# Four of sixteen rows that one DMA engine loads alone are spread over four engines

## Chip, cores, metric

One core of one Trainium2 chip. The metric is the device time of one execution in microseconds (us), median of several executions. Faster or slower needs 2%; for anything smaller I give the ratio of the runs with its 95% interval.

## The reference, cut to what matters

The program is a decode step for four tokens: `x + A(xn) + B(xn)` with `xn = layernorm(x)`. A is attention over a window of 2048 positions of a key and value cache (16 KV heads, 67 MB of keys and values). B ends in a two-layer MLP, and only its last product matters here:

```python
h2 = _gelu(_layernorm(x1, axis=-1) @ w3) @ w4     # w3: 576 x 4608, w4: 4608 x 576, bfloat16
return x1 + h2
```

Everything is read once: 87 MB from HBM for four rows of output.

## The kernel before: the parts concerned

The MLP's hidden vector is contracted over w4's 4608 rows. 4480 rows sit in a tile of 35 slices with 128 partitions, loaded over all 16 DMA engines (16 increments of each piece's semaphore in the trace). The last 128 rows (from `X0`) are split off into a tile x and loaded with few partitions on purpose, so that only some DMA engines work on them (in the trace the semaphore of the load of 20 partitions rises five times, that of the 12 three times, that of a one-partition load once). One row is 576 x 2 = 1152 bytes. A V block is one of the 16 loads of the value cache.

```python
XB, XC, XA = 0, 4, 5          # column slots of the x tile: 4 slots for B, 1 for C, 5 for A
XS, NX = 10, 20

def x4_rows(part):
    t = w_tiles["x4"]
    if part == "A":            # 100 rows: 20 partitions x 5 rows
        src = B_w4[X0 + 28:F, :].rearrange("(q g i) n -> g q (i n)", q=4, g=5)
        nc.sync.dma_start(out=t[0:NX, XA * D:XS * D], in_=src)
    elif part == "C":          # 12 rows: 12 partitions x 1 row
        src = B_w4[X0 + 16:X0 + 28, :].rearrange("(q g) n -> g q n", q=4)
        nc.sync.dma_start(out=t[0:12, XC * D:XA * D], in_=src)
    else:                      # 16 rows in pieces of ONE partition (q), rows lo to hi of its four
        q, lo, hi = part
        src = B_w4[X0 + 4 * q + lo:X0 + 4 * q + hi, :].rearrange("(q i) n -> q (i n)", q=1)
        nc.sync.dma_start(out=t[q:q + 1, (XB + lo) * D:(XB + hi) * D], in_=src)

# which pieces are issued after which V block:
X_AFTER = {13: ["A", (0, 0, 4)], 14: [(1, 0, 4), (2, 0, 2), "C"], 15: [(2, 2, 4), (3, 0, 2), (3, 2, 4)]}
...
# the end of the program on TensorE (cut)
mlp_extra(XC, XS)              # 12 matmuls on x (slots C and A), before the last V block
for s in range(NSL):
    pv(hl, s)                  # last V block
... o_turn, o_sum, o_spread, o_pick ...
mlp_extra(XB, XC)              # 8 matmuls on x: the 16 rows
o_proj(hl)
for lo, hi in pieces:          # w4, six pieces of 18, 6, 5, 4, 1, 1 slices
    mlp_out(lo, hi)
```

## Time and profile before

| | before |
|---|---|
| time, median (three runs) | 211.94 us (211.3 to 212.01) |
| profiled run, span | 211.41 us, 209.6 us |
| share of DMA engines, whole span | 97.7% for the one data queue |
| busiest compute engine | PE, 72% |
| last landing of w4's last piece | 206.60 us |
| copy of the result starts | 206.96 us |

The DMA engines hardly rest (a share of 1.00 or 1.01 from 100 to 204 us), so the time is set by when the last of them has landed its last byte, and by the few matmuls and the store after that. The trace lists every DMA packet with start, duration and bytes, but not its engine. In this document a **train** is a sequence of packets linked by their times, each starting 3 to 4 ns before the record of the one ahead of it ends; there are 16, and I take each for one engine. "Lowest" and "second" to "fifth" are my names for the five trains with x rows, the lowest being the one with the one-partition loads and the fifth the one with the 20-partition load alone; the trace doesn't number engines. Sums of trains are my working from these records, not rows of the profile's page.

### The profile page before, as it was taken

Reading aid. Unit: us, or ns where it says so; the run is one execution under the profiler, and the core shown is the slowest. Engines: PE = TensorE matmul, PEld = TensorE weight load, DVE = VectorE, ACT = ScalarE, POOL = GpSimd, SP = SyncE. Lnnn points to the kernel's source line nnn. Section 1 sums busy time; section 2 is a strip of 40 time slices with the busy share of each in tenths; the row PEclk is TensorE's granted clock in tenths of the full one; section 3 lists DMA queues with packets and bytes.
Section 4 is the critical chain, followed back from the end, with each engine's and each line's share of the span. In section 5 each row is a group of like instructions: output and inputs, shape, how many; then the busy total and the mean of one; then the engine's idle time right before and its main releaser. Section 6 shows DMA issues by size and latency. Waiting matters only on the chain.

```text
span 209.6 us, 2356 instructions
## 1 busy us (share of the span) xinstructions
PE 150.2 (72%) x958; PEld 58.2 (28%) x972; DVE 113.4 (54%) x156; ACT 34.8 (17%) x72; POOL 9.0 (4%) x32
## 2 busy tenths in 40 slices
PE   0357297699590039958998987589697955999693
PEld 0122132233140003213444332234232312343361
DVE  4511877894910083935608889176848390764200
ACT  7612201012010011110222221102111111023100
POOL 4710000000000000000002100000000000000000
PEclk9999589999787555788999999789978796699979
DMA  7999999999999999999999999999999999999992
GB/s 301 400 419 425 425 424 430 438 432 424 434 450 406 427 435 420 443 428 435 428 428 435 419 428 434 435 425 438 428 428 438 415 439 435 416 441 428 432 403 98
DMA packets 6702, 87.31 MB, mean 417 GB/s; under 512 B 758, under 2 KB 1034, under 8 KB 1700
## 3 DMA queue, kind: packets, MB, share of 16 engines
q1 hardware_dynamic: 6684, 87.17, 97.7%
q8 instruction: 7, 0.11, 0.2%
q10 hardware_dynamic: 8, 0.00, 0.0%
q14 instruction: 3, 0.02, 0.0%
HBM read 87.17 MB, written 0.00 MB: 416 GB/s over the span
## 4 chain that ended last, share of the span: by engine, by line
DMA 66%; DVE 15%; PE 14%; ACT 1%; issue 1%; SPq 1%; DVEq 0%; ACTq 0%
DMA kn<-in_A_k_cache_dram 43%; DVE kt L253 12%; DMA vn<-in_A_v_cache_dram 10%; DMA w_sb<-in_B_w_dram 7%; DMA wq_sb<-in_A_wq_dram 6%; PE S L366 5%; PE g_ps L496 2%; PE q_ps L310 2%; PE O L423 1%; PE oT L436 1%; DVE PT L400 1%; PE acc L212 1%; DVE mx L372 1%; PE S L388 1%; ACT E L395 1%
## 5 line engine op out<-in xcount | busy, mean ns | idle before, releaser
L366 PE MATMUL S<-kt,qz 128*128 128x512 bf16 x242 | 76.4, 437 | 32.2 <-DVE kt L253 30.4
L253 DVE STREAM_TRANSPOSE kt<-kn 128x2048 int32<-128x2048 int32 x32 | 73.4, 2297 | 24.3 <-DMA kn<-in_A_k_cache_dram 22.9
L366 PEld LDWEIGHTS <-qz 128*128 128x128 bf16 x256 | 23.5, 106 | 64.3 <-issue 47.7
L423 PE MATMUL O<-vn,PT 128*32 128x512 bf16 x256 | 23.9, 414 | 9.3 <-DMA vn<-in_A_v_cache_dram 9.3
L430 ACT ACTIVATE O_sb<-O,rd 128x512 f32<-128x512 f32 x16 | 11.0, 686 | 64.7 <-DVE rd L413 48.3
L395 ACT ACTIVATE E<-S 128x512 bf16<-128x512 f32 x16 | 9.5, 597 | 72.6 <-PE S L388 72.6
L400 DVE STREAM_TRANSPOSE PT<-E 128x512 bf16<-128x512 bf16 x16 | 11.4, 710 | 14.4 <-ACT E L395 14.4
L446 DVE TENSOR_REDUCE on<-oT 128x8 bf16<-128x128 f32 x16 | 4.6, 289 | 22.1 <-PE oT L436 21.9
L423 PEld LDWEIGHTS <-PT 128*32 128x32 bf16 x256 | 5.5, 95 | 33.0 <-issue 22.1
L436 PE MATMUL oT<-ident_w,O_sb 128*128 128x128 f32 x64 | 12.7, 331 | 0.3 <-ACT O_sb L430 0.3
L372 DVE TENSOR_REDUCE mx<-S 128x1 f32<-128x512 f32 x16 | 10.5, 659 | 1.1 <-PE S L366 1.1
L436 PEld LDWEIGHTS oT<-ident_w,O_sb 128*128 128x128 f32 x64 | 8.3, 165 | 5.2 <-issue 4.3
L388 PE MATMUL S<-nm,j_row 8*128 8x512 bf16 x16 | 6.7, 421 | 1.8 <-DVE nm L384 1.7
L354 PE MATMUL S<-negbig,ohT 4*128 4x512 bf16 x16 | 6.2, 384 | 0.0
L212 PE MATMUL acc<-w_sb,gT 128*4 128x288 bf16 x70 | 5.5, 311 | 0.6 <-DMA w_sb<-in_B_w_dram 0.6
L310 PE MATMUL q_ps<-wq_sb,xnT 128*32 128x512 bf16 x40 | 4.3, 611 | 2.2 <-DMA wq_sb<-in_A_wq_dram 2.2
L212 PE MATMUL acc<-wo_sb,op 128*4 128x288 bf16 x64 | 5.5, 324 | 0.4 <-DVE op L468 0.4
L496 PE MATMUL g_ps<-w_sb,ln2T 128*32 128x512 bf16 (+2 forms) x55 | 5.5, 441 | 0.0
L212 PEld LDWEIGHTS <-gT 128*4 128x4 bf16 (+3 forms) x90 | 4.2, 89 | 3.1 <-issue 1.0
L538 POOL TENSOR_TENSOR g_u<-g_x 128x180 f32<-128x180 f32 x1 | 0.5, 486 | 101.9 <-ACT g_x L532 101.9
L681 DVE CAST fin<-acc 4x288 bf16<-4x288 f32 x1 | 0.4, 446 | 8.1 <-PE acc L212 8.1
L534 DVE COPY g_x<-gT_ps 128x64 f32<-128x64 f32 x2 | 0.4, 223 | 7.5 <-PE gT_ps L518 7.5
(94 smaller groups left out, 79.3 us busy)
## 6 DMA issues: line engine op xcount, KB each, us to landing
kn<-in_A_k_cache_dram SPq DMA_DIRECT2D x16, 2048.0 KB, 25.9
vn<-in_A_v_cache_dram SPq DMA_DIRECT2D x16, 2048.0 KB, 22.7
wo_sb<-in_A_wo_dram SPq DMA_DIRECT2D x4, 1152.0 KB, 37.8
w_sb<-in_B_w_dram SPq DMA_DIRECT2D x1, 4608.0 KB
wq_sb<-in_A_wq_dram SPq DMA_DIRECT2D x1, 4096.0 KB
w_sb<-in_B_w_dram SPq DMA_DIRECT2D x1, 2592.0 KB, 11.0
w_sb<-in_B_w_dram SPq DMA_DIRECT2D x2, 576.0 KB, 34.3
w_sb<-in_B_w_dram SPq DMA_DIRECT2D x1, 864.0 KB
```

Of the source, the lines that this page charges most:

```text
L212: nc.tensor.matmul(out=acc_of(i), lhsT=lhsT, rhs=rhs[:, i * CW:(i + 1) * CW], start=False, stop=False, skip_group_check=True)
L253: nc.vector.transpose(out=kt[:], in_=src)
L310: nc.tensor.matmul(out=q_ps[r][g * QD:(g + 1) * QD, :], lhsT=xnT[:, k, :], rhs=wq_sb[:, col:col + NW], start=(j == 0), stop=False, skip_gr ...
L366: nc.tensor.matmul(out=S_ps[h][:], lhsT=qz[:, z0:z0 + P], rhs=kt[:, ib, c0:c0 + SC, e:2 * QD:2].rearrange("p c k -> p (c k)"), start=False ...
L372: nc.vector.reduce_max(out=mx[:], in_=S_ps[h][:], axis=AX.X)
L388: nc.tensor.matmul(out=S_ps[h][:], lhsT=j_row[:], rhs=st.pop(("nm", h))[:, 0:1].to_broadcast([NJ, NW]), start=False, stop=False, skip_grou ...
L395: nc.scalar.activation(out=E[h][:].rearrange("p c k -> p (c k)"), in_=S_ps.pop(h)[:], func=ACT.Exp, scale=scale, accum_out=st["rs"][:, h % ...
L400: nc.vector.transpose(out=PT[h][:], in_=E.pop(h)[:])
L423: nc.tensor.matmul(out=O_ps[h][g * QD:(g + 1) * QD], lhsT=PT[h][:, c, :], rhs=vn[:, :, c, :], start=(s == 0), stop=False, skip_group_check ...
L430: nc.scalar.activation(out=O_sb[h][:], in_=O_ps.pop(h)[:], func=ACT.Copy, scale=st.pop(("rd", h)))
L436: nc.tensor.transpose(out=oT[:, s, :], in_=o[:, s, :], identity=ident_w[:, s * NJ:s * NJ + P])
L496: nc.tensor.matmul(out=out, lhsT=ln2T[:, k, :], rhs=rhs, start=(j == 0), stop=False, skip_group_check=True)
```

## The change

Intent: the 16 rows ride on one engine only. Four of them (the last row of each partition) shall come by a single load over four engines, one row each, so that the lowest engine has less to do.

```diff
+        elif part == "B":
+            src = B_w4[X0:X0 + 16, :].rearrange("(q i) n -> q i n", q=4)[:, 3]
+            nc.sync.dma_start(out=t[0:4, (XB + 3) * D:XC * D], in_=src)
...
-    X_AFTER = {13: ["A", (0, 0, 4)], 14: [(1, 0, 4), (2, 0, 2), "C"], 15: [(2, 2, 4), (3, 0, 2), (3, 2, 4)]}
+    X_AFTER = {13: ["A", (0, 0, 3)], 14: [(1, 0, 3), "B", "C"], 15: [(2, 0, 3), (3, 0, 1), (3, 1, 3)]}
```

## The prediction

> **What bounds the kernel now.** I read the page's shares first, then its rows over the span, then the table by stretches, the chain of waits, the issue order of the DMA queue, and last the trace's single packet records.
>
> ```profile
> PE 150.2 (72%) x958; PEld 58.2 (28%) x972; DVE 113.4 (54%) x156; ACT 34.8 (17%) x72; POOL 9.0 (4%) x32
> DMA  7999999999999999999999999999999999999992
> DMA packets 6702, 87.31 MB, mean 417 GB/s; under 512 B 758, under 2 KB 1034, under 8 KB 1700
> q1 hardware_dynamic: 6684, 87.17, 97.7%
> q8 instruction: 7, 0.11, 0.2%
> ```
>
> No compute engine is above 72%, while the row of DMA shares is 9 in every slice but the first and the last: one queue's packets fill 97.7% of 16 engines' time over the span. The same by stretches (columns: stretch, its length, busy time of PE, PEld, DVE, ACT, POOL, granted clock, share of the 16 DMA engines, GB/s):
>
> ```profile
> 100.00:140.00 40.00, 34.61 (x250) 14.38 (x248) 24.52 (x31) 7.77 (x24) 2.30 (x5) 0.96 1.01 430
> 140.00:180.00 40.00, 30.91 (x161) 11.07 (x164) 24.70 (x33) 5.50 (x12) 0.00 (x0) 0.85 1.01 430
> 180.00:204.00 24.00, 21.86 (x209) 10.28 (x212) 10.58 (x20) 4.12 (x8) 0.00 (x0) 0.89 1.00 424
> 204.00:206.00 2.00, 1.39 (x22) 0.77 (x18) 0.00 (x0) 0.00 (x0) 0.00 (x0) 1.00 0.82 316
> 206.00:209.60 3.60, 0.93 (x12) 0.44 (x11) 0.45 (x1) 0.40 (x1) 0.00 (x0) 0.92 0.02 7
> ```
>
> From 100 to 204 us the DMA share is 1.00 or 1.01; then it falls to 0.82: some engines have run out of work while others still have some. That ragged last stretch is the only place where moving bytes between DMA engines can pay. The chain of waits agrees (columns: start, duration, what):
>
> ```profile
> 167.94 21.71 DMA vn<-in_A_v_cache_dram
> ...
> 191.35 14.53 DMA w_sb<-in_B_w_dram
> 205.88 0.04 issue
> 205.92 1.05 PE acc L212 x12
> 206.97 0.43 DVE fin L681
> ```
>
> The end is the landing of w4's last pieces, a few matmuls, one copy, and the store. The 16 rows in question are part of x, the small tile that holds w4's last 128 rows; this is who reads it and when:
>
> ```profile
> L212 PE MATMUL acc<-x,gT x20: 278/280/282, 193.0 to 198.2; 20*4 20x288 bf16 x10, 4*4 4x288 bf16 x8, 12*4 12x288 bf16 x2
> L171 SPq DMA_DIRECT2D x<-in_B_w_dram x6: 226/242/426, 164.2 to 185.3; - x6
> ```
>
> The 16 rows come by six loads of one partition each, issued from 164.2 to 185.3 us. The eight matmuls that read them run at 197.86 to 198.5 us (timeline), so what matters is not when these rows land but which DMA engine spends time on them.
>
> **The packet records.** The trace gives start, duration and bytes of every packet, but not its engine. On one engine the next packet starts about 4 ns before the record of the last one ends (after a 4-byte completion packet, 3 ns), so I linked packets into 16 trains by these ends. A few ties of 1 ns leave which train is which uncertain; the times at which trains end are certain. Three readings:
> - All 16 trains run from about 2 us to their ends with next to no gap. Each DMA engine is therefore busy throughout, and its end is the sum of its packets.
> - The last eight-packet piece of w4 (1152 B a row) ends between 204.45 and 206.30 us over the 16 trains, a spread of 1.85 us. The last seven ends are 206.08, 206.08, 206.09, 206.12 or 206.13, 206.21 and 206.30, within the uncertainty of the ties.
> - The train with the one-partition loads (packets of 4608 B at 183.43 and 188.47 us, 2304 B at 188.65, 193.80, 193.90 and 193.99) ends, as I link it, at 206.21: second to last. The train that ends at 206.30 has none of the x rows in it.
>
> The last increments of the last piece's semaphore come at 206.43, 206.51, 206.51 and 206.60 us, 0.30 us after the trains' ends; the matmuls that wait for it start at 206.64. So the end is set by a train at 206.30 that isn't the one which the change relieves, with the relieved one 0.09 us ahead of it.
>
> [...] the load of 20 partitions from 5 groups shows as 4 packets of 5760 B on each of five trains, the one of 12 partitions as 4 packets of 1152 B on each of three, and the one-partition loads lie in one train. So the new load, 4 partitions from 4 groups, should put one packet on each of four engines. [...] here a 16384-byte packet recurs every 607 ns, 27.0 GB/s[...]. [...] the trace shows seven such packets on queue 8, of 0.88 to 1.00 us where data packets of that size take 0.61. They are load on engines that the kernel didn't plan, and no part of the change.
>
> **The change, part by part.** Bytes, matmuls and the x tile's layout stay the same. There are eight x loads before and eight after, and comparing the instruction orders shows everything outside the DMA queue unchanged but for line numbers. On the DMA queue the loads stand in the same places; each of them and of w4's six loads still waits for the completion of the one eight places earlier.
>
> Removed from the lowest engine: two packets of 4608 B and four of 2304 B. Their pitches are 174 and 89 ns (a 178 ns or 93 ns record less the 4 ns overlap): 2 x 174 + 4 x 89 = 704 ns. Added: three rows at a time three times (3456 B; a line through 1152 B at 47 ns and 4608 B at 174 ns gives 132 ns), two rows once (89), one row once (47), and its row of the spread load (47): 3 x 132 + 89 + 47 + 47 = 579 ns. Completion packets: six before, six after. So the lowest engine is relieved of **125 ns**. This is three rows' worth and not four, because the spread load gives one row back.
>
> Added on the next three engines: one packet of 47 ns and one completion packet of about 6 ns net, **+53 ns each**. These are trains with the 20-partition load; I link their ends at 205.58, 205.95, 206.08 and 206.13 at the latest, so 206.18 at most afterwards. Those are still ahead of 206.30.
>
> Sum on the path: the relieved train goes from 206.21 to about 206.09, the three others to at most 206.18, the last stays at 206.30. The time won is **0**. If ties misled me and the relieved train was the last one, the gain would be the 0.09 us down to the next. After the last landing, 209.59 - 206.60 = 2.99 us follow unchanged.
>
> **Rivals.** (a) *The lowest engine sets the end and the full relief shows*: -0.13 us, 211.8. For: it carries 40 extra rows (16 + 4 + 20), some 1.9 us more than engines with none. Against: its train isn't last in this trace, and others lie within 0.1 to 0.2 us. (b) *The spread load creates a wait*: it completes when four engines have reached it rather than one, and w4's third load waits for that completion. For: engines are up to 1.8 us apart. Against: its predecessor landed at 188.7 us, w4's third load is issued at 190.9, and the packets of that load don't start before about 202 us; even 5 us late would be covered. 211.9. (c) *The queue's issue time grows*: the 12-partition load took 0.82 us to issue, one-partition loads about 0.24 (median). At most 0.6 us more on a queue that stands waiting for 4.6 us next to it, and whose transfers are queued several us ahead. 211.9. (d) *One of the three loaded engines becomes last*: +0.05 us at most, 212.0. (e) *Run-to-run drift*: the three runs span 211.3 to 212.01, 0.7 us, several times any of these.
>
> **Range and chances.** The predicted time is 211.9 us: the median of before with a change of 0 to -0.1. The mechanism can give only -0.13 to +0.05, so the range comes from the spread of the runs, widened a little for another chip: 211.2 to 212.5. A change of 2% would be 4.2 us, thirty times what the moved packets weigh. Within 2%: 0.98; faster 0.01; slower 0.01.
>
> **What would show it right or wrong.** Right: DMA shares of 9 throughout; four packets of 1152 B at about the same time on four trains, three of 3456 B on one; that train ending some 0.12 us earlier relative to the others; the last landing at 206.6 within a few tenths and 3.0 us after it. Wrong: a gap in the trains around 185 to 195 us, a longer wait of the DMA queue on the new load's line, matmuls on x later than 198 us, or a last landing that moves by over half a microsecond with the train of the one-partition loads as its cause.

What is cut there (marked) gave a rule for how a load is shared out over engines, a rated speed of one engine and a mechanism for the instruction packets; no trace of this case shows these. The sum came to 0 us won, with 0.125 us less on the lowest engine and 0.053 us more on each of the next three. That the new load puts one packet on each of four engines rests on the pattern of the loads of 20 partitions in five groups, 12 in three and of one, on five, three and one trains. The "seven such packets" are the seven of 16384 bytes that the page gives as `q8 instruction`.

## The result, and the profile after

| | before | after |
|---|---|---|
| time, median of six runs each | 211.34 us (211.07 to 212.01) | 211.31 us (211.13 to 211.79) |
| profiled run, span | 211.41, 209.6 us | 211.31, 209.5 us |
| last landing of w4's last piece | 206.60 us | 206.54 us |
| copy of the result starts | 206.96 us | 206.90 us |

The ratio is 0.9994, 95% interval 0.9974 to 1.0015: no difference. (A ratio is the mean time of one kernel's fast runs over the mean of the other's of the same rounds, so not quite the ratio of the medians in the table.)

The page of the kernel after, DMA shares and packets:

```profile
DMA  7999999999999999999999999999999999999992
DMA packets 6708, 87.31 MB, mean 417 GB/s; under 512 B 761, under 2 KB 1042, under 8 KB 1706
```

The shares are as before, digit for digit. There are six packets more: six data packets have become nine, and the load over four engines brings four completion packets where a one-partition load had one. The table by stretches (columns as in the prediction) and the chain of waits, after:

```profile
204.00:206.00 2.00, 0.93 (x14) 0.55 (x15) 0.00 (x0) 0.00 (x0) 0.00 (x0) 1.00 0.76 294
206.00:209.60 3.60, 0.86 (x12) 0.40 (x8) 0.45 (x1) 0.40 (x1) 0.00 (x0) 0.87 0.01 5
```

```profile
166.64 22.96 DMA vn<-in_A_v_cache_dram
...
191.30 14.51 DMA w_sb<-in_B_w_dram
205.81 0.04 issue
205.85 1.06 PE acc L215 x12
206.91 0.43 DVE fin L684
```

The same chain with every step within 0.07 us from w4's landing on. The ragged last stretch, where some engines have finished and others haven't, is still there (share 0.76 against 0.82). Who reads the x tile, after:

```profile
L215 PE MATMUL acc<-x,gT x20: 278/280/282, 192.8 to 199.2; 20*4 20x288 bf16 x10, 4*4 4x288 bf16 x8, 12*4 12x288 bf16 x2
L174 SPq DMA_DIRECT2D x<-in_B_w_dram x5: 240/249/427, 164.0 to 185.3; - x5
L167 SPq DMA_DIRECT2D x<-in_B_w_dram x1: 248/248/248, 170.0 to 170.0; - x1
```

Five one-partition loads and one load over four partitions (L167), which cost the queue 0.248 us to issue, 0.022 more than the piece it replaced (0.226).

The packets show the mechanism at work. Two engines can be told by their packets, and I follow their trains from the first packet of the 20-partition load to the end of the last w4 packet: the lowest one (it alone has the one-partition pieces), and, in the kernels with a spread load, the fourth (it has a packet of the spread load, and none of the 12-partition load). Ties of 1 ns leave second ways open; for the lowest train before, one would end at 206.116, but without its 2304-byte packet of 193.993 us. In the kernel before, the fourth isn't marked: two trains have a part of the 20-partition load and none of the smaller x loads. One of them, which starts at 182.639, has a 20736-byte packet of 1047 ns instead of 771. In the seven traces with a spread load that were linked, such a packet (1047 to 1061 ns) lies in the fifth train, the one with the 20-partition load alone; so I take the other one for the fourth.

| train | kernel | first x packet | end | length |
|---|---|---|---|---|
| lowest | before | 182.557 | 206.212 | 23.655 us |
| lowest | after | 182.422 | 205.949 | 23.527 us |
| fourth | before (taken for it) | 183.373 | 206.093 | 22.720 us |
| fourth | after | 183.447 | 206.220 | 22.773 us |

The lowest train is shorter by 0.128 us and the fourth longer by 0.053 us. The fourth is now the last of all 16; of the 0.127 us by which it ends later, 0.053 are the new row and 0.074 its later start in this run. So the relief is real and worth nothing: the engine that got relief wasn't the last one, and in this trace one that paid for it is. A landing is signalled about 0.3 us after its train's end (0.27 to 0.32 in eight traces here, 0.46 in one, that of the x rows early).

### The profile page after: what moved, and what is told of

It is laid out like the page before. It is cut to its first block, busy times and chain, and to the rows that moved or that the text cites. A ratio compares the mean times of both kernels' runs of the same rounds, so it can differ in the third digit from the quotient of the medians.

```text
span 209.5 us, 2370 instructions
## 1 busy us (share of the span) xinstructions
PE 150.2 (72%) x972; PEld 57.8 (28%) x972; DVE 113.3 (54%) x156; ACT 34.9 (17%) x72; POOL 9.0 (4%) x32
## 2 busy tenths in 40 slices
DMA packets 6708, 87.31 MB, mean 417 GB/s; under 512 B 761, under 2 KB 1042, under 8 KB 1706
## 4 chain that ended last, share of the span: by engine, by line
DMA 76%; PE 18%; DVE 3%; ACT 1%; SPq 1%; issue 1%; DVEq 0%; ACTq 0%
DMA vn<-in_A_v_cache_dram 51%; DMA kn<-in_A_k_cache_dram 12%; DMA w_sb<-in_B_w_dram 7%; DMA wq_sb<-in_A_wq_dram 6%; PE S L369 6%; PE O L426 3%; PE g_ps L499 2%; DVE kt L256 2%; PE q_ps L313 2%; PE oT L439 1%; PE acc L215 1%; PE S L391 1%; DVE qz L345 1%; PE gT_ps L521 1%; SPq L153 1%
## 5 line engine op out<-in xcount | busy, mean ns | idle before, releaser
L369 PE MATMUL S<-kt,qz 128*128 128x512 bf16 x256 | 77.6, 432 | 31.6 <-DVE kt L256 31.6
L215 PE MATMUL acc<-w_sb,gT 128*4 128x288 bf16 x70 | 4.9, 286 | 1.1 <-DMA w_sb<-in_B_w_dram 1.1
L215 PE MATMUL acc<-wo_sb,op 128*4 128x288 bf16 x64 | 4.6, 286 | 0.4 <-DVE op L471 0.4
L240 PE MATMUL tp<-ident_bf,first 4*128 4x4 bf16 x8 | 0.6, 172 | 5.3 <-DVE first L227 5.3
```

The source lines that it names most:

```text
L215: nc.tensor.matmul(out=acc_of(i), lhsT=lhsT, rhs=rhs[:, i * CW:(i + 1) * CW], start=False, stop=False, skip_group_check=True)
L369: nc.tensor.matmul(out=S_ps[h][:], lhsT=qz[:, z0:z0 + P], rhs=kt[:, ib, c0:c0 + SC, e:2 * QD:2].rearrange("p c k -> p (c k)"), start=False ...
```

## Experiments

**Theory.** The end follows the slowest of 16 trains, and these are nearly even: relieving one wins nothing, loading one costs as soon as it becomes the slowest. **Rivals:** the lowest engine's train alone sets the end; or only the sum of bytes counts. Later a third came up: TensorE, not DMA, sets the end in some runs. All experiments start from the changed kernel; their ratios are to the kernel before of the same rounds.

**The changed kernel again.** No edit.

> The changed kernel once more, as the null for the runs beside it. Slowest-train theory (the last of 16 DMA trains sets the end, and the lowest engine's isn't it): ratio to before 0.999 to 1.001, last landing at 206.4 to 206.7 us. Lowest-engine theory (the relieved train sets the end): 0.9994, a difference of 0.13 us, which time alone can hardly separate from the other; so the trace is to say where the train with the 3456-byte packets ends (205.95 us in the first trace of this kernel, 0.26 us ahead of the last train).

Measured: 211.33 us (211.10 to 212.02, five runs), ratio 0.9998 (0.9985 to 1.0012). The profiled run was the slow one, 212.02. Its lowest train is 23.528 us long and its fourth 22.773, the same as in the first trace to a nanosecond, and the fourth, at 206.365, is again the last by far; the last two increments of the last piece's semaphore come at 206.280 and 206.668 us. So the two lengths are properties of the kernel, and where a train stands when its x packets begin is what varies, by 0.1 to 0.2 us between these traces.

This run is 0.7 us slower than the first trace's, and the later landing gives only 0.13 of it. TensorE's order of time after the last V block has landed, and the table by stretches, first for the changed kernel's quick run (211.31 us), then for this one (212.02 us); columns of the first: start, duration, engine, line, what, and in brackets the idle time before and what ended it:

```profile
194.66 1.59 PE L426 MATMUL O<-vn,PT 128*32 128x512 bf16 x16 [0.99 <-DMA vn<-in_A_v_cache_dram]
...
200.89 3.11 PE L215 MATMUL acc<-w_sb,gT 128*4 128x288 bf16 x48
204.44 0.78 PE L215 MATMUL acc<-w_sb,gT 128*4 128x288 bf16 x10 [0.44 <-DMA w_sb<-in_B_w_dram]
205.85 1.02 PE L215 MATMUL acc<-w_sb,gT 128*4 128x288 bf16 x12 [0.63 <-DMA w_sb<-in_B_w_dram]
206.90 0.45 DVE L684 CAST fin<-acc 4x288 bf16<-4x288 f32 x1 [7.04 <-PE acc L215]
```

```profile
194.00:204.00 10.00, 8.57 (x104) 5.33 (x105) 1.43 (x4) 0.69 (x1) 0.00 (x0) 0.83 0.98 410
```

```profile
194.75 1.90 PE L426 MATMUL O<-vn,PT 128*32 128x512 bf16 x16 [1.43 <-DMA vn<-in_A_v_cache_dram]
...
200.34 2.08 PE L215 MATMUL acc<-wo_sb,op 128*4 128x288 bf16 x16
202.22 5.32 PE L215 MATMUL acc<-w_sb,gT 128*4 128x288 bf16 x70
207.57 0.45 DVE L684 CAST fin<-acc 4x288 bf16<-4x288 f32 x1 [7.29 <-PE acc L215]
```

```profile
194.00:204.00 10.00, 8.87 (x72) 4.72 (x74) 1.43 (x4) 0.69 (x1) 0.00 (x0) 0.50 0.97 410
```

In the quick run TensorE had half its clock for 3.4 us of this stretch (mean 0.83), ran ahead of w4's pieces and waited for DMA twice. In the slow run it had half its clock from 193.7 to 204.0 us, as the trace's clock record says (mean 0.50); then its 70 matmuls on w4 run in one piece without a wait, and the copy starts 0.90 us after the last landing instead of 0.36. There the end of the program is TensorE's. This trace's half-clock stretches last 3.413, 6.827, 10.240 or, once, 17.067 us, one to five times 3.413 (the last stretch is cut off by the end), and where they fall differs from run to run: in the quick run the one in this stretch lies from 195.02 to 198.43 us.

**Seventeen more rows on the lowest engine.**

```diff
+        elif part == "E":      # 17 partitions: in the trace all 17 packets on one train
+            src = B_w4[0:17, :].rearrange("(q i) n -> q (i n)", q=17)
+            nc.sync.dma_start(out=t[0:17, XS * D:(XS + 1) * D], in_=src)
...
-    ... 15: [(2, 0, 3), (3, 0, 1), (3, 1, 3)]}
+    ... 15: [(2, 0, 3), (3, 0, 3), "E"]}
```

> The changed kernel plus one load of 17 rows that goes to one engine alone: 17 packets of 1152 B at 47 ns, 0.80 us more on the lowest engine (two other pieces are merged so that the number of loads stays). Slowest-train theory: the lowest train goes from about 205.95 to 206.75 us and becomes the last; with the others at 206.2 to 206.3 the time rises by 0.4 to 0.6 us, ratio 1.002 to 1.003. Bytes theory (only the sum of bytes over 16 engines counts): 19.6 KB at 430 GB/s are 0.05 us, ratio 1.000. Lowest-engine theory: the full 0.80 us, ratio 1.004.

Measured: 212.22 us (212.01 to 212.42), ratio 1.0045 (1.0033 to 1.0058), +0.93 us in the medians. The lowest train is 24.323 us long, 0.796 more than in the changed kernel, as worked out, and is the last at 207.139 us, far from the next landing:

```profile
191.11 15.60 DMA w_sb<-in_B_w_dram
206.71 0.04 issue
206.76 1.05 PE acc L218 x12
207.81 0.43 DVE fin L687
```

The bytes theory is out: 19.6 KB, 0.02% of the traffic, cost 0.45% of the time. The size of my slack was wrong: I had taken 0.3 us between the lowest train and the last from one trace of the changed kernel, and in this run the lowest train's x packets began 0.39 us later than there (182.816), so nothing was left of it. Whether that is so in all five runs, which lie close together, the one trace can't say. By its size this result fits the lowest-engine theory just as well; the next run decides.

**No x rows at all** (wrong result: the tile is zeroed, no load of the 128 rows is issued).

```diff
+        nc.gpsimd.memset(w_tiles["x4"][0:NX, 0:XS * D], 0.0)
...
-    X_AFTER = {13: ["A", (0, 0, 3)], 14: [(1, 0, 3), "B", "C"], 15: [(2, 0, 3), (3, 0, 1), (3, 1, 3)]}
+    X_AFTER = {13: [], 14: [], 15: []}
```

> The changed kernel without any of the loads of the last 128 rows of w4; the tile is set to zero, so the result is wrong on purpose. The lowest engine is relieved of 37 rows, about 1.8 us, the next four of 1.0 to 1.25 us. Slowest-train theory: the trains that carry an instruction block and none of these rows still end at 206.1 to 206.3, so the time falls by 0 to 0.1 us, ratio 0.9995 to 1.000. Bytes theory: 147 KB at 430 GB/s, 0.34 us less, ratio 0.998. Lowest-engine theory: it falls until the next train, several tenths at least, ratio 0.997 or less.

Measured: 211.13 us (211.05 to 211.60), ratio 0.9998 (0.9985 to 1.0010). Taking 37 rows off the lowest engine and 147 KB off the whole brought nothing that five rounds can see. The 16 increments of the last piece's semaphore, one for each engine, in us (from the trace's semaphore records):

```
before        204.81 204.96 205.08 205.14 205.91 206.17 206.21 206.34 206.36 206.37 206.40 206.42 206.43 206.51 206.51 206.60
after         204.56 204.62 204.77 205.03 205.70 206.12 206.13 206.21 206.21 206.24 206.25 206.35 206.40 206.41 206.51 206.54
no x rows     204.90 204.93 204.96 204.97 205.00 205.02 205.20 205.65 205.78 206.22 206.38 206.47 206.57 206.60 206.61 206.80
four16_again  204.50 204.58 204.68 204.91 206.11 206.12 206.17 206.17 206.18 206.23 206.27 206.28 206.33 206.34 206.38 206.74
```

Without the x rows five engines have moved to 205.8 us or earlier, and the last seven stand at 206.2 to 206.8; those of before stand at 206.4 to 206.6. The instruction queue carries seven packets of 16 KiB in this trace, as in that of before, and seven is also the number of late engines. My links put the seven packets into different late trains, but over that length ties make single links uncertain. What is certain: the x rows fill the low engines up to where seven engines end anyway. This excludes the lowest-engine theory.

**All sixteen rows over four engines.**

```diff
+        elif part in ("B0", "B1", "B2"):
+            i = int(part[1])
+            src = B_w4[X0:X0 + 16, :].rearrange("(q i) n -> q i n", q=4)[:, i]
+            nc.sync.dma_start(out=t[0:4, (XB + i) * D:(XB + i + 1) * D], in_=src)
...
+    X_AFTER = {13: ["A", "B0"], 14: ["B1", "B", "C"], 15: ["B2"]}
```

> The change carried to its end: all 16 rows come by four loads over four engines. Against the changed kernel the lowest engine loses another 0.40 us (579 + 36 ns of packets and completions become 4 x 53), the next three gain 3 x 53 = 0.16 us each. Slowest-train theory: the three end at up to 206.2 + 0.16, the rest where they were: the time changes by 0 to +0.15 us, ratio 1.000 to 1.001. Lowest-engine theory: 0.5 us less than before, ratio 0.9975.

Measured: 211.92 us (211.43 to 212.15), ratio 1.0029 (1.0016 to 1.0041). Slower by more than I allowed. The last train ends at 206.422 us. It has packets of the four spread loads and of the 12-partition load, so it is the second or third engine's; the fourth train ends at 206.071. The profiled run (212.02) was again one with half clock up to 203.8 us, so that the copy started at 207.48, 0.77 us after the last landing. A mix of both, then.

> The 16 rows over four engines once more, unchanged. If the first result was chance (more runs with an unlucky half-clock stretch), the runs fall into two groups near 211.4 and 212.0 and the ratio comes down, 1.000 to 1.002. If the four loads cause it, 1.002 to 1.004 again.

Measured: 211.76 us (211.57 to 211.79), ratio 1.0009 (0.9990 to 1.0028). In this trace the fourth train is 22.931 us long, 0.211 more than the 22.720 taken for it before; worked out were 4 packets of 47 ns with 4 completions of 6 ns, 0.212. It ends at 206.415 us, and as the last row of the list above shows, its increment comes 0.36 us after the fifteenth. TensorE waits for it as in the quick run:

```profile
190.40 15.59 DMA w_sb<-in_B_w_dram
205.99 0.04 issue
206.03 1.08 PE acc L219 x12
207.11 0.44 DVE fin L688
```

So with the change carried further, one of the three trains that it loads is the slowest in both traces, by 0.33 and 0.36 us. The two results (1.0029 and 1.0009) have overlapping intervals; that the time rises by about the 0.2 us of the train is likely, not shown by the times alone.

**The x rows early** (an attempt at a better version): all x loads go ahead of the last V load, and their last eight matmuls move to the wait before the last V block.

```diff
-    X_AFTER = {... 14: [(1, 0, 3), "B", "C"], 15: [(2, 0, 3), (3, 0, 1), (3, 1, 3)]}
+    X_AFTER = {... 14: [(1, 0, 3), "B", "C", (2, 0, 3), (3, 0, 1), (3, 1, 3)], 15: []}
...
-    mlp_extra(XC, XS)
+    mlp_extra(XB, XS)
...
-    mlp_extra(XB, XC)
```

> The changed kernel with all loads of the small tile ahead of the last V load, and its eight late matmuls done with the other twelve, before the last V block's matmuls. Tail theory (the end is the later of two: the last DMA landing, or TensorE's chain from the last V landing, which a half-clock stretch from 194 to 204 us makes 0.67 us longer than the DMA, as in the profiled run of 212.02 us): the eight matmuls, 0.65 us at full and 1.12 us at half clock, fall into a wait of TensorE of 1.0 to 1.4 us; runs near 212.0 go away, the quick ones stay: all runs within 211.0 to 211.6, ratio to before 0.997 to 1.000. Slowest-train theory alone: nothing changes, the spread of the runs stays at 211.1 to 212.0.

Measured: 211.65 us (211.22 to 212.08, six runs), ratio 1.0006 (0.9985 to 1.0027). The matmuls did move into the wait, but the runs near 212 stayed, so the tail theory isn't the whole of the spread. The profiled run was 212.08, and it was slow by DMA:

```profile
192.73 1.39 PE L215 MATMUL acc<-x,gT 4*4 4x288 bf16 x20
194.59 1.41 PE L426 MATMUL O<-vn,PT 128*32 128x512 bf16 x16 [0.47 <-DMA vn<-in_A_v_cache_dram]
...
206.56 1.02 PE L215 MATMUL acc<-w_sb,gT 128*4 128x288 bf16 x12 [0.62 <-DMA w_sb<-in_B_w_dram]
```

One train without any x row ended at 206.80 us, 0.55 after the next; its landing came at 207.26 us, the fifteenth at 206.57. It is the train with the instruction block of 198.63 us, and the packet behind that block took 1321 ns instead of 771. But the packets behind this block lost about as much in the quick run (724 and 354 ns instead of 262 each), so why the train fell behind in this run I can't say. The same reordering with all sixteen rows over four engines:

> The 16 rows over four engines in four loads, with the same reordering. Tail theory: the 0.63 us that the 16 rows over four engines cost came from TensorE's chain at half clock, so it shrinks to the DMA share, 0 to 0.2 us: ratio 0.998 to 1.001. If the four-engine loads themselves cost it (three trains longer, loads issued earlier), the ratio stays at 1.002 to 1.004.

Measured: 211.60 us (211.34 to 212.00, six runs), ratio 1.0006 (0.9985 to 1.0026). The ratio lies where the tail theory put it, but the same version without the reordering had 1.0009 in the same rounds, so the reordering isn't shown to be the cause. In the trace (211.60 us) the fourth train is 22.931 us long again and the last, at 206.353. Neither version beats the kernel before.

**Sixty-eight more rows on the lowest engine.** As with seventeen, but four rows for each of the 17 partitions.

> The changed kernel plus one load of 68 rows (17 packets of 4608 B at 174 ns, 78 KB) on one engine alone: 2.96 us more on the lowest engine. Slowest-train theory: the lowest train goes from about 205.95 to 208.9 us, 2.6 to 2.7 us past the others; time +2.5 to +2.8 us, ratio 1.012 to 1.013, and a last stretch of nearly 3 us with one engine in sixteen busy. Bytes theory: 0.18 us, ratio 1.001. If the lowest engine had slack of its own beyond what the trains show, less than 2.5 us.

Measured: 216.39 us (215.80 to 216.62, four runs), ratio 1.0223 (1.0203 to 1.0243): +4.6 us, far more than the 2.5 to 2.8 expected. The direction is that of the theory, the size isn't. The table by stretches and the chain of waits of this run:

```profile
194.00:200.00 6.00, 4.34 (x56) 2.50 (x57) 1.43 (x4) 0.69 (x1) 0.00 (x0) 1.00 0.99 389
206.00:209.00 3.00, 3.00 (x28) 1.70 (x26) 0.00 (x0) 0.00 (x0) 0.00 (x0) 0.50 0.12 47
```

```profile
189.56 15.48 DMA w_sb<-in_B_w_dram
205.05 0.04 issue
205.09 7.10 PE acc L218 x70
212.19 0.43 DVE fin L687
```

Two things add up. First, of the 17 packets the first eight took 178 ns and the other nine 181 to 384, so the load took 4.13 us instead of 2.96, and in the same moments some 40 packets of other engines were slowed too (over 776 ns instead of 771; the first line shows 389 GB/s, where the kernel before moved 413). The last landing came at 210.95 us, 4.3 us later than usual. Second, w4's first piece, 36 of the last 70 matmuls, waits for the same engine and landed at 205.05 instead of 200.6; all 70 matmuls came after it, and with half the clock for much of that time (0.50 in the second line) they took 7.1 us, so the copy began 1.2 us after the last landing instead of 0.4. My expectation had priced a late train by its end alone; it also delays every piece before the last, and with them TensorE.

Why the packets were slow I tried to settle with other source rows, then other destination partitions.

```diff
-            src = B_w4[0:68, :].rearrange(...)
+            src = B_w4[X0 - 68:X0, :].rearrange(...)          # low68_far
-            nc.sync.dma_start(out=t[0:17, ...], in_=src)
+            nc.sync.dma_start(out=t[8:25, ...], in_=src)      # low68_shift (source rows as at first)
```

> The 68-row load on the lowest engine again, now of rows of w4 other than those which all engines read at that moment. If reading the same region slowed the packets (nine of 17 took 181 to 384 ns instead of 178, and some 40 of the big packets on other engines more than 776 instead of 771): all 17 take 178 ns, the lowest train is 2.96 us longer, the last landing comes at 206.6 + 2.7 = 209.3 us and the time is 2.7 us more at full clock, up to 3.6 if TensorE runs the last 70 matmuls at half clock; ratio 1.013 to 1.017. If the slow packets have another cause: 1.022 as before.

Measured: 215.89 us (215.50 to 216.23), ratio 1.0206 (1.0183 to 1.0230), and the same durations again: eight of 178 ns, then 315, 315, 182, 305, 376, 340, 213, 294, 406. The source rows aren't the cause.

> The 68-row load once more, from the first rows again, but written to partitions 8 to 24 instead of 0 to 16. In both earlier runs the packets for partitions 0 to 7 took 178 ns and the nine after them 181 to 406, in the same pattern. If the destination partition decides, the slow pattern (about 313, 314, 181, 324, 384, 349, 219, 295, 382) comes with the first nine packets now. If it is the moment (the ninth packet and later, from about 195.3 us), the first eight take 178 ns again and the next nine are slow. The time is 215 to 217 us in either case.

Measured: 216.68 us in one run (before: 211.41). Now the first four took 178 ns, and the next thirteen 319, 315, 186, 327, 382, 351, 214, 306, 398, 366, 211, 315, 380. Neither expectation: partitions 8 to 11 were slow before and are quick here, the slow packets begin with the fifth instead of the ninth, and at 194.6 us instead of 195.2 to 195.5. Taken in order of partitions, the slow packets come in fours in all three runs, begin at a partition divisible by four (8, 8 and 12), and the third of each four is the quickest (181 and 219, 182 and 213, 186, 214 and 211 ns). What slows them stays open; which other engines wrote to the same partitions just then wasn't looked at.

**512 more rows over all 16 engines.** Again the same edit with `q=128` partitions and four rows each.

> The changed kernel plus one load of 512 rows (128 packets of 4608 B, 590 KB) over all 16 engines: 8 packets of 174 ns and a completion, 1.40 us more on every engine. Slowest-train theory and bytes theory both expect +1.4 us (590 KB at 430 GB/s are 1.37 us), ratio 1.0065; it is here to set 7.5 times the bytes of the 68-row run beside that run: if only the slowest train counts, these bytes cost half as much. If DMA weren't the bound at all, 0 for both.

Measured: 212.82 us (212.57 to 212.93, four runs), ratio 1.0056 (1.0039 to 1.0074); the last landing came at 208.06 us, 1.4 to 1.5 later than the 206.54 and 206.67 of the changed kernel's two traces. The load shows as 142 packets more than the changed kernel has (6850 against 6708): 128 of data and 16 completions, less two of a merged piece. So 590 KB over all engines cost 1.1 us and 78 KB on one engine 4.6 (of which, from the numbers above, some 1.2 are the slow packets and 0.9 TensorE's later copy). This confirms DMA as the bound, and that it is a bound by engine.

**The 128 rows loaded like all others**, over all 16 engines (right result; w4 as 36 slices, no x tile).

```diff
-    NFM = NF - 1
+    NFM = NF
-            n = NFH - e
+            n = NFH
-    mlp_extra(XC, XS)
-    mlp_extra(XB, XC)
     (and the x columns of the hidden vector dropped from the transposes)
```

> The last 128 rows of w4 are loaded like the others, one per partition over all 16 engines, and multiplied by two matmuls instead of twenty; no separate tile; the result is right. The five low engines are relieved of all x rows (1.0 to 1.8 us), every engine gets 8 x 1152 B more in packets that grow from 6912 to 8064 B, 8 x 42 = 0.34 us. Slowest-train theory: the trains with an instruction block end 0.34 us later, time +0.25 to +0.35 us, ratio 1.001 to 1.002. Bytes theory: the same bytes, ratio 1.000. Lowest-engine theory: a gain of 0.5 us or more, ratio 0.9975.

Measured: 211.74 us (211.52 to 211.84), ratio 1.0005 (0.9992 to 1.0018). By time undecided between +0.15% and nothing. By trace as expected: the first nine increments of the last piece come between 205.23 and 206.00 us, the last seven between 206.60 and 207.04; the last seven come 0.24 to 0.38 us later than without x rows, about the 0.34 us of their share, and the five relieved ones don't count.

## Why the prediction was right

**DMA engines as the bound**: right. Shares, gapless trains and the 512-row run agree; in two traces (the changed kernel again, and all sixteen rows over four engines for the first time) TensorE at half clock comes last instead, by 0.4 to 0.5 us, which the prediction didn't see. It had noted a wait of TensorE for w4's last pieces, but not how short it is: 0.6 us.

**The lowest engine is relieved of 125 ns**: right. 23.655 - 23.527 = 0.128 us, and 0.127 in the second trace.

**The next three get 53 ns each**: right where it could be followed, on the fourth engine: 22.773 - 22.720 = 0.053, and 4 x 53 in the run with four such loads (0.211). The before value rests on which train I take for the fourth.

**Which train is last**: here a step failed without consequence. The prediction had "the three others to at most 206.18, the last stays at 206.30", from one trace of before. In five traces with spread loads (the changed kernel twice, all sixteen rows over four engines three times) the last train is one of the three that these loads lengthen, at 206.22 to 206.42: the fourth in four of them, the second or third in one. With the x rows early the fourth is second, at 206.25. That is rival (d), priced at +0.05 us at most. The order of trains within 0.3 us changes from run to run, and one trace was too little to say which is last. The sum is 0 to 0.05 us either way, which intervals of 0.3 to 0.4 us to either side don't resolve.

**Rival (a)**, the lowest engine alone: excluded by the run without x rows, which took 37 rows off it for 0.9998. **Rival (b)**, a wait for the spread load's completion: no such wait; w4's third load was issued at 190.83 us after, 190.88 before. The spread load did complete later: its four increments come at 188.64 to 189.68 us, where the piece it replaced landed at 189.15 (the prediction's 188.7 is the end of its packet). That leaves 1.15 us. **Rival (c)**, issue time: 0.248 us for the new load, 0.226 for the old. **Rival (e)**, drift: two sources found, a half-clock stretch of TensorE over the tail and a straggling train, each worth 0.5 to 0.7 us in one run; the share of each over all runs isn't known.

**A sign of being wrong that came true**: the prediction named matmuls on x later than 198 us, and the last eight ran from 198.87 us (before: 197.86). The rows aren't the cause, they had landed by 194.8; TensorE had half its clock from 195.02 to 198.43 us in this run, and only from 198.75 on in the trace of the kernel before. The end didn't feel it, since TensorE still waited for w4 afterwards.

**The time**: 211.9 predicted, 211.31 measured, in the range; the kernel before came down by as much with three more runs (211.94 to 211.34), so the 0.6 us are drift and not the change.

## What to carry to other kernels

Where the DMA engines have no gaps, ask of a load not how many bytes it moves but which engines carry it and whether one of them is the last to finish; relief for another engine was worth nothing here (0.128 us of it, ratio 0.9994), and load on the last cost in full (0.80 us more in its train, 0.93 us in time), with 68 rows also through what waited on its earlier pieces. Before balancing by hundreds of bytes, see how far the order of the engines' ends changes between runs: here by 0.3 us, more than the 0.13 at stake. And TensorE, which waited for DMA by only 0.6 us, was a second bound here: in the two traces where its clock was 0.50 to 0.52 up to 204 us it came last, by 0.4 to 0.5 us.

## What else the packets and the clock record showed

- 16384-byte packets follow each other every 607 ns, 27.0 GB/s, and 1152-byte ones every 47 ns, 24.5 GB/s. A fixed part of some 5 ns for each packet and 0.0368 ns for each byte fit the sizes 1152 and 4608 (47 and 174 ns).
- How many engines a load used here: 17 partitions put all 17 packets on one train, 4 on four trains, 12 (from 3 groups) on three, 20 (from 5 groups) on five.
- One load of 17 packets of 4608 B had packets of up to 406 ns instead of 178, and some 40 packets of other engines were slow in the same 3 us; neither the source rows, nor the destination partition, nor the place in the load explained it alone.
- Seven blocks of 16 KiB on the instruction queue took 0.88 to 1.00 us each, where a data packet of that size takes 0.61; in the traces before and after, 15 data packets are under way for most of a block's time instead of 16. The data packet right behind the last block (it starts 4 to 5 ns before the block's record ends) was slow as well: 725 ns before and 724 after, instead of 262. With no x rows at all, seven engines' landings come at 206.2 to 206.8 us and nine at 205.8 or earlier; that these seven are the ones with an instruction block is likely from my links, not certain.
- In the slow run of the changed kernel TensorE worked from 194.75 us on with no pause over 0.4 us (busy 8.87 of the 10 us from 194 on) and still had half its clock until 203.97 us, the end of a half-clock stretch of 10.24 us.
